# Spectral and dense layers on one core: another layout of a scratch tensor in memory, and an earlier place for one piece of the inverse transform

## The chip, the core and the metric

The kernel runs on one core of a Trainium2 chip. A core has five engines that run side by side and synchronise by semaphores: TensorE (PE, matrix products; its weight loads are shown apart as PEld), VectorE (DVE), ScalarE (ACT), GpSimd (POOL) and SyncE (SP), which only issues DMAs. Data move between the on-chip memory (SBUF, 128 partitions) and the main memory by 16 DMA engines; SP, ACT and POOL each have a queue to issue DMAs on. TensorE writes its results to PSUM, eight banks, from which DVE or ACT copy them out. The metric is the device time of one execution in microseconds; several executions are timed and the median is compared.

## What is computed

Two kinds of layer alternate, each twice: a spectral layer A and a dense layer B, both on a normalised input and added to it.

```python
def _A_ref(x, w_r, w_i):
    X = rfft2(x.astype(float32), axes=(-2, -1))
    X = X * (w_r + 1j * w_i)
    return irfft2(X, s=(S, D), axes=(-2, -1)).astype(bfloat16)

def _B_ref(x, w1, b1, w2):
    h = einsum("bsd,df->bsf", x, w1) + b1
    sp = log1p(exp(-abs(h))) + where(h > 0, h, 0)
    return einsum("bsf,fd->bsd", h * tanh(sp), w2)

x = A_x
x = x + _A_ref(_layernorm(x), A_w_r, A_w_i)
x = x + _B_ref(_layernorm(x), B_w1, B_b1, B_w2)
x = x + _A_ref(_layernorm(x), A_w_r, A_w_i)
x = x + _B_ref(_layernorm(x), B_w1, B_b1, B_w2)
```

S is 2048 rows, D 1024 columns, the hidden width of the dense layer 3584; data are bfloat16. `h * tanh(sp)` is the Mish function, which ACT computes in one instruction.

## The kernel before

**Order of work.** The program is written out by hand: each engine has one list of instructions, in the order in which the Python code adds them, and a helper (`op`, `group`, `dma`) works out which semaphores an instruction must wait for from the buffers that it reads and writes. An engine works strictly in its list's order, so an instruction that waits holds all that stand behind it, DMA issues included. The activations stay in SBUF (`XS`, 16 tiles of 128 rows).

**The spectral layer** (`layer_A`) computes both Fourier transforms as matrix products with constant tables. After a first stage the frequencies are worked through in eight groups g; `order_A` gives the order of the stages of all groups, several groups in flight at once. For each group, s2 and s3 finish the forward transform and apply the filter, i1 and i2 begin the inverse one. i2 leaves the group's result in the buffer `U[g % 3]`: 128 partitions (index l, the place in a piece of 128 columns), and in each partition 16 components r by 128 values n. That is 4 KB per partition, 512 KB per group.

The last step of the inverse transform, `i4`, contracts over all 128 components (16 of each of the eight groups), so these must lie on partitions, and l and n in a partition. The turn from the one order to the other is made through main memory, by the scratch tensor `u_scratch` (`u_d`), made in `build` at L309:

- `u_turn` (L864 to L877) stores a group. Groups 0 to 6 go as a whole on SP's queue once both halves of i2 are done (L875); group 7 goes in two halves of eight components each on ACT's queue (L871), so that the first half is on its way while the second is computed.
- `u_back` (L886 to L890) reads a group back into `UT`, one component per partition: component r of group g comes to partition 8 r + g. It is issued on SP, one group behind the stores: after the store of group g, the load of group g - 1. The load of group 6 is issued at the first half of group 7 (L870).
- `u_last` (L892 to L901) reads group 7 back in six parts: the first half's eight components in two parts of 64 values of l on SP, the second half's in four parts of 32 values of l, in turn on ACT and SP. Each part waits for the store of its half.

In the layout before, `u_scratch` has the order (group, l, r, n): a store writes 4 KB (group 7: 2 KB) per partition in one contiguous piece, and a load gathers pieces of 128 values, 256 bytes, into each component's partition.

While group 7 makes this way, TensorE has only `spin(4, 0)` (L940), matmuls whose result isn't used, and `residual_first` (L998), which puts the first four tiles of `XS` into PSUM. Behind the loads on SP stand the first loads of the dense layer's weights (`load_w1`, L1041), which wait for `UT` to be complete.

**The dense layer** (`layer_B`) starts with i4. For the first four row tiles, four calls of 32 values of l each (L1186; matmuls of 128x32, line L1014) add to the residual in PSUM, `out_first` (L1019) copies the sums to `XS` on ACT, and DVE takes the statistics of the normalisation. For the other twelve row tiles the work is cut into small pieces: `rest(bank, n)` (L1168) makes n matmuls of 128x96 (also line L1014) into PSUM banks from `bank` on, and one copy from there to the staging buffer `YS`, on ACT (line L568) unless told otherwise. These pieces stand between the dense layer's own matmuls. The first tiles are normalised (`apply`, L505, on DVE), transposed on TensorE (`transposed`, L1056: eight transposes at L1069 into bank 6 or 7, one copy out on DVE at L1074), and multiplied with w1 (`mm1`, L1088, matmuls at L1103 into banks 0 to 2), with the Mish on ACT (L1107). `self.warm(ACT.Mish)` (L1198) is a tiny activation whose purpose is to load ACT's table for Mish early. The second product, with w2, is `mm2` (L1113, line L1121).

The order at the start of the dense layer is: `rest(0)`, two `apply`, two `transposed`, the warming of the table, `rest(3)`, and further on the first `mm1`.

Of the kernel before, what the change touches and what calls it, by code (L numbers as in the profile page):

```python
# [7 lines left out]
P = 128  # L8
BF = dt.bfloat16
# [165 lines left out]
def to_bf16_bits(a):  # L175
    u = np.ascontiguousarray(a, dtype=np.float32).view(np.uint32).astype(np.uint64)
    return np.ascontiguousarray((((u + 0x7FFF + ((u >> 16) & 1)) >> 16) & 0xFFFF).astype(np.uint16))


class KB:  # L180
# [122 lines left out]
    def build(self):  # L303
        nc = self.nc
        tabs = make_tables()
        con = {k: nc.inline_tensor(to_bf16_bits(v), name=f"c_{k.lower()}") for k, v in tabs.items()}
        self.con = {k: v.ap().bitcast(BF) for k, v in con.items()}
        self.con["IDF"] = nc.inline_tensor(np.eye(P, dtype=np.float32), name="c_idf").ap()
        self.u_d = nc.dram_tensor("u_scratch", (8, P, 16, P), BF, kind="Internal").ap()  # L309
        self.w_d = nc.dram_tensor("w_scratch", (8, P, 2, 2, 512), BF, kind="Internal").ap()  # L310
        self.xn_d = nc.dram_tensor("xn_scratch", (16, P, self.D), BF, kind="Internal").ap()
        from contextlib import ExitStack
        with ExitStack() as es:
            def sb(name, shape, dtype=BF):
                return es.enter_context(nc.sbuf_tensor(name, [P] + shape, dtype))

            sb("PAD0", [64])
            self.XS = sb("XS", [16, self.D])
            self.IDENT = sb("IDENT", [P])
            self.M = sb("M", [P])  # L320
            self.MT = sb("MT", [P])
            self.FD = sb("FD", [5 * 512])
            self.BD = sb("BD", [13 * P])
            self.B1 = sb("B1", [self.NF], F32)
            self.B1h = sb("B1h", [self.NF])
            self.BN = sb("BN", [16, 12], F32)
            self.MV = sb("MV", [16, 2], F32)
            self.RS = sb("RS", [4, 16], F32)
            self.EPS = sb("EPS", [32], F32)
            sb("PAD1", [32])  # L330
            self.PS = es.enter_context(nc.psum_tensor("PS", [P, 8, 512], F32))
            self.PSb = self.PS[:].bitcast(BF)
            self.arena_bytes = nc.sbuf_bytes_remaining // 64 * 64 - 64
            self.ARENA = es.enter_context(nc.sbuf_tensor("ARENA", [P, self.arena_bytes // 2], BF))
            self.r_bank = [Res(f"bank{i}") for i in range(8)]
            self.r_xs = [Res(f"XS{i}") for i in range(16)]
            self.r_mv = [Res(f"MV{i}") for i in range(16)]
            self.r_rs = [Res(f"RS{i}") for i in range(16)]
            self.r_ident, self.r_m, self.r_mt, self.r_fd, self.r_bd = (Res(n) for n in ("id", "m", "mt", "fd", "bd"))
            self.r_b1, self.r_eps, self.r_warm = Res("b1"), Res("eps"), Res("warm")  # L340
            self.r_ud = [Res(f"ud{i}") for i in range(8)]
            self.r_ud7 = [Res(f"udh{i}") for i in range(2)]
            self.r_wd = [Res(f"wd{i}") for i in range(8)]
            self.r_xnd = [Res(f"xnd{i}") for i in range(16)]
            self.npair = 0
            self.W1_OFF = self.arena_bytes - 4 * 4096
            self.layout()
            self.prologue()
            self.layer_A(0)
            self.layer_B(0, last=False)  # L350
            self.layer_A(1)
            self.layer_B(1, last=True)
            self.dma_wait_all()
            for p in (self.pe, self.dve, self.act, self.sp, self.pool):
                p.sem = es.enter_context(nc.semaphore(name=f"sem_{p.name}"))
            for d_ in self.dsems.values():
                d_.sem = es.enter_context(nc.semaphore(name=d_.name))
            self.block = es.enter_context(nc.Block())
            self.flush()
# [329 lines left out]
    def layer_A(self, li):  # L689
# [7 lines left out]
        dve, act, sp, pool = self.dve, self.act, self.sp, self.pool  # L697
# [166 lines left out]
        def u_turn(g, half):  # L864

            u = U[g % 3]
            if g == 7:
                h = slice(8 * half, 8 * half + 8)
                if half == 0:
                    u_back(6)  # L870
                self.dma(act, self.u_d[g][:, h, :], u.ap[:, h, :], f"uwh{half}", reads=[u.res], writes=[self.r_ud7[half]])  # L871
                if half:
                    u_last()
            elif half:
                self.dma(sp, self.u_d[g], u.ap, f"uw{g % 3}", reads=[u.res], writes=[self.r_ud[g]])  # L875
                if g:
                    u_back(g - 1)  # L877

        def open_ut():
            self.UT = self.alloc("UT", o["UT"], [P, P])  # L880

            self.r_ut = self.sub_res(self.UT, "ut", 4, o["UT"], P * P * 2)
            for r in self.r_ut:
                r.begin()

        def u_back(g):  # L886
            if self.UT is None:
                open_ut()
            self.dma(sp, self.UT.ap[g:P:8, :, :], self.u_d[g].rearrange("l r n -> r l n"), f"usp{g % 3}",
                     reads=[self.r_ud[g]], parts=self.r_ut)  # L890

        def u_last():  # L892

            def back(prog, half, q, n):
                l = slice(32 * q, 32 * q + 32 * n)
                self.dma(prog, self.UT.ap[7 + 64 * half:P if half else 64:8, l, :], self.u_d[7][l, 8 * half:8 * half + 8, :].rearrange("l r n -> r l n"),
                         f"ul{half}{q}", reads=[self.r_ud7[half]], parts=self.r_ut[q:q + n])
            back(sp, 0, 0, 2)
            back(sp, 0, 2, 2)
            for q in range(4):  # L900
                back((act, sp)[q % 2], 1, q, 1)  # L901
# [147 lines left out]
    def layer_B(self, li, last):  # L1049
        pe, dve, act, sp, pool = self.pe, self.dve, self.act, self.sp, self.pool  # L1050
# [117 lines left out]
        def rest(bank, n=15, prog=act):  # L1168

            u0 = self.u0  # L1170
            self.u0 += n
            self.i4(4, 12, u0, n, bank)
            self.i4_out(4, 12, u0, n, bank, staged=YS, prog=prog)
# [17 lines left out]
            self.out_first(u, 2, (act, act, act, dve)[u])  # L1191
        self.root(0, 2)
        rest(0)
        for j in range(2):
            xn[j] = self.apply(j)
        for j in range(2):
            transposed(0, j, xn[j])
        self.warm(ACT.Mish)  # L1198
        rest(3)
        at_tiles(0)  # L1200
        for j in (2, 3):
            self.stats_dve(j)
# [118 lines left out]
```

## Time and profile before

| | us |
|---|---|
| median of 8 runs | 1014.73 |
| fastest and slowest of them | 1014.37, 1015.99 |
| the profiled execution, as timed | 1014.61 |
| its span from the first to the last instruction | 1012.8 |
| PE busy in it | 958.5 (95%) |
| ACT, DVE, POOL busy | 347.6, 326.6, 81.7 |
| first spectral layer's last i4 input landed, about | 114.5 |
| second spectral layer's, about | 604.9 |

How the scratch tensor's DMAs stand in the page (engine whose queue issues them, number, size of each, median time from issue to landing):

```profile
u_scratch<-ARENA SPq DMA_DIRECT2D x14, 512.0 KB, 4.0
ARENA<-u_scratch SPq DMA_DIRECT2D x14, 512.0 KB, 6.1
...
u_scratch<-ARENA ACTq DMA_DIRECT2D x4, 256.0 KB, 3.9
```

`ARENA` is the one SBUF tensor in which all buffers of the layers lie, `U` and `UT` among them. In the timelines a row gives start, duration, engine, line, operation, tiles, shapes and number of instructions, and in brackets how long the engine was idle before it and what ended the wait. In the chain of waits each piece is followed back from what came last. Rows on stretches of time give the busy time of each engine in the stretch, the clock that was granted to TensorE as a share of the full one, the busy share of the DMA engines (packets can overlap, so it can pass 1) and the rate in GB/s.

### The profile page before, as it was taken

The page shows a single profiled execution, that of the slowest core. Times are in us where ns is not written, and L with a number is a line of the kernel's source. Part 1 is how long each engine was busy: PE and PEld are TensorE (multiplying, and loading weights), DVE is VectorE, ACT ScalarE, POOL GpSimd, SP SyncE. Part 2 cuts the span into 40 slices and gives each one's busy share as a digit, 9 for nine tenths or more (in the row PEclk, how much of TensorE's full clock was granted, in tenths as well). Part 3 has the DMA queues.
Part 4 walks back from the last instruction along what each step waited for, and adds up shares of the span by engine and source line. Part 5 has one row for each costly group of instructions (what it writes and reads, how often), then busy time and mean ns, then how long its engine had stood idle before and what let it go on. Part 6 is the DMA issues. An engine that isn't in the chain of part 4 may idle for free.

```text
span 1012.8 us, 13752 instructions
## 1 busy us (share of the span) xinstructions
PE 958.5 (95%) x5826; PEld 506.8 (50%) x5826; DVE 326.6 (32%) x679; ACT 347.6 (34%) x487; POOL 81.7 (8%) x114
## 2 busy tenths in 40 slices
PE   1799799999999999999999979999999999999998
PEld 0676575444444444444456748644444444444443
DVE  6797468002443000033347736820011100000111
ACT  7898474330000334300029837533100023430000
POOL 4831000000000000003421100000000000000000
PEclk9999899999999999999999998999999999999999
DMA  9969813662111220002922875246411212100000
GB/s 284 295 187 319 216 47 115 208 197 55 46 46 32 81 75 21 1 21 93 194 57 90 237 178 152 78 163 201 129 25 48 70 52 83 43 1 11 21 27 26
DMA packets 154205, 107.00 MB, mean 106 GB/s; under 512 B 74448, under 2 KB 133664, under 8 KB 154144
## 3 DMA queue, kind: packets, MB, share of 16 engines
q1 hardware_dynamic: 143056, 78.61, 27.4%
q0 software_dynamic: 8912, 25.84, 8.6%
q10 hardware_dynamic: 2176, 1.66, 0.5%
q8 instruction: 47, 0.77, 0.3%
q14 instruction: 14, 0.11, 0.0%
HBM read 80.85 MB, written 20.71 MB: 100 GB/s over the span
## 4 chain that ended last, share of the span: by engine, by line
PE 87%; DVE 5%; DMA 4%; ACT 3%; issue 0%; SPq 0%; POOL 0%; ACTq 0%; DVEq 0%
PE PS L1121 38%; PE PS L1103 38%; PE PS L793 2%; PE PS L719 2%; PE PS L1014 2%; PE PS L818 2%; DMA ARENA<-c_bt 1%; ACT ARENA L441 1%; DMA ARENA<-u_scratch 1%; PE PS L1069 1%; DVE ARENA L637 1%; DMA u_scratch<-ARENA 1%; DMA XS<-in_A_x_dram 1%; DVE ARENA L610 1%; DVE ARENA L775 1%; ACT ARENA L635 1%
## 5 line engine op out<-in xcount | busy, mean ns | idle before, releaser
L1103 PE MATMUL PS<-ARENA 128*128 128x512 bf16 (+1 forms) x1984 | 390.9, 358 | 0.1
L1121 PE MATMUL PS<-ARENA 128*128 128x512 bf16 x1792 | 387.4, 379 | 0.0
L1107 ACT ACTIVATE ARENA<-PS,B 128x512 bf16<-128x512 f32 (+1 forms) x248 | 159.3, 645 | 411.5 <-PE PS L1103 411.0
L1103 PEld LDWEIGHTS PS<-ARENA 128*128 128x128 bf16 x1984 | 193.1, 98 | 192.5 <-DVE ARENA L1074 0.7
L1121 PEld LDWEIGHTS PS<-ARENA 128*128 128x128 bf16 x1792 | 175.3, 98 | 211.5
L1132 DVE TENSOR_TENSOR XS<-PS,XS 128x512 bf16<-128x512 f32 x63 | 43.6, 692 | 582.1 <-PE PS L1121 582.1
L460 DVE BATCH_NORM_STATS2 BN<-XS 128x6 f32<-128x512 bf16 x99 | 63.8, 674 | 5.4 <-DMA XS<-in_A_x_dram 4.3
L249 POOL DMA_DIRECT2D xn_scratch<-ARENA x12 | 6.5, 541 | 373.7 <-DVE ARENA L512 373.7
L793 PE MATMUL PS<-ARENA 128*128 128x256 bf16 x256 | 32.4, 273 | 4.0 <-DVE ARENA L782 3.2
L771 ACT ACTIVATE ARENA<-PS 128x1024 bf16<-128x1024 f32 x32 | 33.3, 1071 | 4.5 <-PE PS L767 4.5
L432 ACT ACTIVATE RS<-MV,EPS 128x2 f32<-128x2 f32 (+2 forms) x5 | 1.5, 298 | 96.6 <-DVE MV L463 84.4
L719 PE MATMUL PS<-FD,ARENA 128*128 128x256 bf16 (+1 forms) x256 | 31.8, 271 | 2.4 <-ACT ARENA L635 1.2
L1014 PE MATMUL PS<-MT,ARENA 128*128 128x32 bf16 (+1 forms) x512 | 22.3, 202 | 10.5 <-DMA ARENA<-u_scratch 7.2
L804 ACT ACTIVATE ARENA<-PS 128x1024 bf16<-128x1024 f32 x28 | 29.8, 1089 | 3.9 <-PE PS L793 3.9
L793 PEld LDWEIGHTS PS<-ARENA 128*128 128x128 bf16 x256 | 24.0, 98 | 12.1 <-DVE ARENA L782 5.8
L568 ACT ACTIVATE ARENA<-PS 128x1440 bf16<-128x1440 f32 (+1 forms) x22 | 25.5, 1160 | 11.0 <-PE PS L793 3.9
L775 DVE TENSOR_TENSOR ARENA<-ARENA 128x1024 bf16<-128x1024 bf16 x32 | 22.0, 688 | 21.2 <-ACT ARENA L771 21.2
L719 PEld LDWEIGHTS PS<-FD,ARENA 128*128 128x128 bf16 x256 | 24.4, 98 | 6.5 <-DVE ARENA L637 1.4
L1014 PEld LDWEIGHTS PS<-MT,ARENA 128*128 128x128 bf16 x512 | 20.8, 104 | 13.4 <-issue 7.9
L818 PE MATMUL PS<-ARENA,BD 128*128 128x256 bf16 x192 | 24.9, 273 | 1.6 <-DVE ARENA L572 1.6
L862 ACT ACTIVATE ARENA<-PS 128x1024 bf16<-128x1024 f32 x24 | 25.3, 1093 | 0.0
L512 DVE TENSOR_SCALAR ARENA<-XS,MV,RS 128x1024 bf16<-128x1024 bf16 x47 | 24.5, 546 | 0.9
(85 smaller groups left out, 531.3 us busy)
## 6 DMA issues: line engine op xcount, KB each, us to landing
ARENA<-in_B_w_dram SPq DMA_DIRECT2D x56, 512.0 KB, 3.9
ARENA<-in_B_w_dram SPq DMA_DIRECT2D x56, 256.0 KB, 4.3
u_scratch<-ARENA SPq DMA_DIRECT2D x14, 512.0 KB, 4.0
ARENA<-u_scratch SPq DMA_DIRECT2D x14, 512.0 KB, 6.1
w_scratch<-ARENA POOLq DMA_DIRECT2D x8, 512.0 KB, 7.0
ARENA<-w_scratch POOLq DMA_DIRECT2D x8, 512.0 KB, 5.4
out_dram<-XS SPq DMA_DIRECT2D x16, 256.0 KB, 2.0
ARENA<-xn_scratch POOLq DMA_DIRECT2D x15, 256.0 KB, 9.4
```

What stands on the lines that cost most here:

```text
L460: self.op(self.dve, lambda e: e.bn_stats(self.BN[:, j, 6 * h:6 * h + 6], self.XS[:, j, 512 * h:512 * h + 512]), reads=[self.r_xs[j]], part ...
L719: fns.append(lambda e: e.matmul(dst, at(r), FD[:, t:t + n], start=start, stop=stop))
L771: self.op(act, lambda e: e.activation(x.ap.rearrange("p a b -> p (a b)"), ps, ACT.Copy, scale=SIG), reads=banks, writes=[x.res])
L775: self.op(dve, lambda e: e.tensor_tensor(ta.ap, x.ap, wt.ap[:, 0:1, :].to_broadcast([P, 2, 512]), ALU.mult), reads=[x.res, wt.res], writes ...
L793: fns.append(lambda e, c=c, part=part: e.matmul(ps[:, c * 256:(c + 1) * 256], yk.ap[:, part, c * P:(c + 1) * P], t[:, (128, 0)[part]:(384, ...
L804: self.op(act, lambda e: e.activation(v.ap[:, :, i, :], src, ACT.Copy), reads=banks, parts=[v.res])
L818: fns.append(lambda e, dst=dst, part=part, c=c: e.matmul(dst, BD[:, c:c + P], mov(kd, part), start=(part == 0), stop=(part == 1)))
L1014: fns.append(lambda e, l=l: e.matmul(self.PS[:, bank + l // k, l % k * w:(l % k + 1) * w], self.UT.ap[:, u0 + l, :], self.MT[:, 8 * lo:8 * ...
L1103: fns.append(lambda e, db=db, bank=bank, fl=fl: e.matmul(PS[:, bank, 0:w], wb.ap[:, db, fl * P:(fl + 1) * P], x.ap[:, db, tok], start=(db ...
L1107: self.op(act, lambda e, bank=bank, ft=ft: e.activation(at.ap[:, ft, tok], PS[:, bank, 0:w], ACT.Mish, bias=self.B1[:, ft:ft + 1]), reads= ...
L1121: fns.append(lambda e, i=i, ft=ft: e.matmul(PS[:, bank, :], at.ap[:, ft, t * P:(t + 1) * P], W2[ft].ap[:, h * 512:(h + 1) * 512], start=(i ...
L1132: self.op(dve, lambda e: e.tensor_tensor(xs, PS[:, bank, :], xs, ALU.add), reads=[self.r_bank[bank]], writes=[self.r_xs[j]])
```

## The change

The scratch tensor gets the order (group, r, l, n): a component's row is contiguous in memory, 32 KB. The stores now scatter each partition's 4 KB (group 7: 2 KB) in pieces of 256 bytes, and the loads read one contiguous piece per component: 32 KB for groups 0 to 6, and for group 7's parts 16 KB (64 values of l) or 8 KB (32 values). Queues, order, waits and the number of DMAs stay as they are. Besides, in the dense layer one `rest(3)` moves from behind the transposes and the warming of the Mish table to a place right behind `rest(0)`.

```diff
@@ build
-        self.u_d = nc.dram_tensor("u_scratch", (8, P, 16, P), BF, kind="Internal").ap()
+        self.u_d = nc.dram_tensor("u_scratch", (8, 16, P, P), BF, kind="Internal").ap()
@@ u_turn
-                self.dma(act, self.u_d[g][:, h, :], u.ap[:, h, :], f"uwh{half}", reads=[u.res], writes=[self.r_ud7[half]])
+                self.dma(act, self.u_d[g][h].rearrange("r l n -> l r n"), u.ap[:, h, :], f"uwh{half}", reads=[u.res], writes=[self.r_ud7[half]])
...
-                self.dma(sp, self.u_d[g], u.ap, f"uw{g % 3}", reads=[u.res], writes=[self.r_ud[g]])
+                self.dma(sp, self.u_d[g].rearrange("r l n -> l r n"), u.ap, f"uw{g % 3}", reads=[u.res], writes=[self.r_ud[g]])
@@ u_back
-            self.dma(sp, self.UT.ap[g:P:8, :, :], self.u_d[g].rearrange("l r n -> r l n"), f"usp{g % 3}",
+            self.dma(sp, self.UT.ap[g:P:8, :, :], self.u_d[g], f"usp{g % 3}",
                      reads=[self.r_ud[g]], parts=self.r_ut)
@@ u_last
-                self.dma(prog, self.UT.ap[7 + 64 * half:P if half else 64:8, l, :], self.u_d[7][l, 8 * half:8 * half + 8, :].rearrange("l r n -> r l n"),
+                self.dma(prog, self.UT.ap[7 + 64 * half:P if half else 64:8, l, :], self.u_d[7][8 * half:8 * half + 8, l, :],
                          f"ul{half}{q}", reads=[self.r_ud7[half]], parts=self.r_ut[q:q + n])
@@ layer_B
         self.root(0, 2)
         rest(0)
+        rest(3)
         for j in range(2):
             xn[j] = self.apply(j)
         for j in range(2):
             transposed(0, j, xn[j])
         self.warm(ACT.Mish)
-        rest(3)
         at_tiles(0)
```

## The prediction

> **What bounds the kernel now.** I read first where the chain that ended last spends its time.
>
> ```profile
> PE 87%; DVE 5%; DMA 4%; ACT 3%; issue 0%; SPq 0%; POOL 0%; ACTq 0%; DVEq 0%
> ```
>
> TensorE is the chain for 87% of the span; what is not TensorE lies mostly in the two spectral layers. The diff touches what their ends hang on: the scratch tensor between L871/875 and L889/896, and the start of the next stage. So I read the chain in order of time there, first layer, then second:
>
> ```profile
> 104.89 3.71 DMA u_scratch<-ARENA
> 108.62 0.67 SPq L249
> 109.34 0.59 SPq L249
> 109.97 4.48 DMA ARENA<-u_scratch
> 114.59 2.63 PE PS L1014 x96
> ```
>
> ```profile
> 596.12 4.01 DMA u_scratch<-ARENA
> 600.15 4.74 DMA ARENA<-u_scratch
> 605.03 3.59 PE PS L1014 x128
> ```
>
> The whole machine waits for group 7's trip through memory: 9.7 us from the first store's issue at 104.89 to 114.59, and 8.9 us from 596.12 to 605.03 (the first store there is issued at 595.06). TensorE has only the spin and the residual matmuls (L646, L1003) to fill it. Next I cut the trip into stretches (time, then busy time of PE, PEld, DVE, ACT and POOL, the granted clock, the busy share of the DMA engines, GB/s):
>
> ```profile
> 100.70:102.30 1.60, 1.00 (x8) 0.70 (x8) 1.14 (x3) 0.28 (x1) 0.00 (x0) 1.00 1.03 307
> 592.80:594.00 1.20, 0.71 (x7) 0.64 (x8) 0.49 (x2) 0.34 (x1) 0.00 (x0) 1.00 1.27 290
> 594.00:596.80 2.80, 2.01 (x28) 1.20 (x25) 1.32 (x2) 1.19 (x2) 0.00 (x0) 1.00 1.24 210
> 106.80:108.60 1.80, 1.74 (x5) 0.53 (x5) 0.00 (x0) 0.00 (x0) 0.00 (x0) 1.00 0.94 303
> 598.70:600.20 1.50, 1.50 (x5) 0.42 (x3) 0.00 (x0) 0.00 (x0) 0.00 (x0) 1.00 0.05 18
> 601.20:604.80 3.60, 0.00 (x0) 0.00 (x0) 0.00 (x0) 0.00 (x0) 0.00 (x0) 0.92 0.64 130
> ```
>
> Row 1 is group 6's store in 4 KB pieces. Rows 2 and 3 are the loads of groups 5 and 6, whose packets are all under 512 B: 290 GB/s at first, then 210. Row 4 is both stores of group 7 (2 KB pieces), which hardly move before 106.8 because group 6's load holds the engines. Row 5 is a straggler: a few packets hold the second layer's stores for 1.5 us. Row 6 is group 7's loads, at 130 GB/s, with the engines only 0.64 busy: each writes eight partitions. The last view is the start of the dense stage, TensorE's timeline:
>
> ```profile
> 118.88 1.38 PE L1014 MATMUL PS<-MT,ARENA 128*128 128x96 bf16 x15 [1.67 <-ACT XS L568]
> 120.44 1.89 PE L1069 MATMUL PS<-IDENT,ARENA 128*128 128x128 bf16 x16 [0.18 <-DVE ARENA L512]
> 122.12 1.19 PE L1014 MATMUL PS<-MT,ARENA 128*128 128x96 bf16 x15
> 123.14 1.91 PE L1103 MATMUL PS<-ARENA 128*128 128x256 bf16 x16
> ```
>
> The second L1014 row is the piece that moves. It now fills the time in which VectorE copies the second transpose out (L1074, 122.36 to 123.05).
>
> **The change, part by part, per layer.** The bytes stay the same; the short pieces (256 B) move from the loads to the stores, and the loads get pieces of 32 KB, 16 KB or 8 KB.
>
> *Group 6's store (SP).* 512 KB take 1.6 us (row 1). No row has 256 B writes into memory, so I bound it by 256 B loads: 1.8 us at 290 GB/s, 4.0 us at 130; the other end is no loss. Row 2 is nearest, since its loads too reach the engines at full share: 1.8 us, +0.2. Queued behind it on SP: group 6's load waits for it, and group 7's loads stand behind that.
>
> *Loads of groups 5 and 6 (SP).* 1 MB from 102.5 to 106.8, 4.3 us. At row 1's rate 3.2 us; at row 3's 210 GB/s throughout 5.0 us. I take 3.9, since the first 1.2 us already run near 290: -0.4. What comes free is the way for group 7's stores.
>
> *Group 7's stores (ACT).* Issue: a store takes 0.33 us on ACT, a load in 256 B pieces 0.58 on SP, so +0.25 for the first and about +0.4 for the second, as ACT's copy at 105.28 sits between. Hidden now: the first store starts moving 1.9 us after its issue, group 6's store 0.9 us after. If that cover goes, it costs the 0.25 to 0.4. Data: 1.8 us now, 1.8 at 290 GB/s, 4.0 at 130; I take +0.1. In the second layer row 5's straggler adds 1.5 us; it follows a load in 256 B pieces that one engine ends late. With long pieces it may vanish (-1.2) or stay, or come from the scattered stores (0); I take -0.7.
>
> *Group 7's loads (SP and ACT).* 512 KB in 3.6 to 3.8 us. They still write eight partitions each, so about half of the engines: half of row 1's rate is 154 GB/s, 3.4 us; half of the 406 GB/s that the input loads reach at 3 to 4 us is 203, 2.6 us; the other end is no gain. I take 3.0, -0.8. SP's four issues of about 0.6 us shrink towards a plain store's 0.32, so the last starts earlier: -0.2 more.
>
> *Overlap.* In the first layer 32 of the 128 matmuls of L1014 run before the last load lands (112.59), in the second none. Shorter late loads should let some of those 0.95 us in: -0.4 in the second layer (0 to -0.95).
>
> *Groups 0 to 5.* Stores +0.2, loads -0.2 each, beside TensorE: nothing. The cover is the ring of three U buffers; without it, the table loads on POOL's queue come later (TensorE waits 0.8 us for one of them now).
>
> *The moved piece.* 15 matmuls with their weight loads and one ScalarE copy move ahead of 2 x 8 transposes; no DMA moves. TensorE has 0.18 us free there and the piece takes 0.64 us at full clock, 0.98 at the half clock granted here, so the transposes come 0.5 to 0.8 us later, the second copy with them, and the first L1103 matmul starts at about 123.7 with TensorE idle in front of it. On ScalarE the piece's copy (1.4 us) goes in front of the Mish table load (1.28 us), which had been hidden under the transposes; it still ends near 124.6, when the first Mish input is ready. Some comes back: at 127.44 TensorE waits 0.28 us for a copy that is now done earlier. Bounds 0 to +0.8, taken +0.4.
>
> **Sum.** First layer: 0.2 - 0.4 + 0.1 - 1.0 + 0.4 = -0.7. Second: the same -0.7, less 0.7 and 0.4: -1.8. Together -2.5. The profiled execution took 1014.61 us (span 1012.8 and 1.8 around it), so 1012.1; the median of the runs, 1014.73, lies 0.1 higher: **1012.2 us**.
>
> [...]
>
> **Rivals.**
>
> *Scattered stores are slow* (the slower side). Place: group 6's and 7's stores, 1 MB on the chain per layer. For it: nothing in the profile writes memory in pieces below 2 KB, and loads in 256 B pieces sank from 290 GB/s to 210 and 130. Against: 256 B is no handicap in row 2. At 130 GB/s the two take 8.0 us in place of 3.4, 4.3 more than my +0.3 per layer: 1012.2 + 8.6 = 1020.8; at 170, 2.5 more: 1017.2. It decides from 1 MB in 4.95 us (3.4 + 0.3 + 1.25), about 210 GB/s: there the gain is gone.
>
> *The loads don't get faster*, held by the partitions that they write, or because the long pieces are cut up again and the change doesn't do what it says. For it: row 3 and row 6 are below row 2 with the same pieces. Then -0.4 and -0.8 fall away twice: 1014.6, no change.
>
> *The granted clock comes back late.* It is 0.50 from 116.2 to 122.9 and from 604.1 to 614.2, and rises 4 us after 118.88 and 610.27, from where TensorE works nearly without a gap. The moved piece opens a gap of 0.7 to 0.9 us in just that stretch. The two cold stretches last 6.7 and 10.1 us, 3.4 apart; if the clock rises 3.4 us later, the dense matmuls lose 1.7 us per layer, the piece its full 0.8: +2.1 per layer, 1016.4.
>
> *Everything at the long pieces' rate*: loads of groups 5 and 6 at 3.2 us (-0.7 more), group 7's at 2.6 (-0.4), straggler gone (-0.5): 1012.2 - 2.7 = 1009.5.
>
> **Chances.** Forecast 0.42 (own range 1010.8 to 1013.8), slow stores 0.27, everything fast 0.12, loads unchanged 0.10, late clock 0.09. About 0.2%, 2.0 us, is what a measurement of this kernel tells from no change, so faster means below 1012.7 and slower above 1016.8. Faster: 0.28 of the forecast, 0.12, 0.01 of the unchanged loads: 0.41. Slower: 0.26 of the slow stores, 0.07 of the clock, 0.04 of the unchanged loads, 0.02 of the forecast: 0.39. The rest, 0.20, is no change. The range runs from 1010.0, which leaves out part of the fast case, to 1019.5, which leaves out stores below about 145 GB/s.
>
> **What would show it.** In the changed profile: the store of group 6 at 290 GB/s and landed about 3.3 us after its issue (now 3.1), or far below; the loads of group 7 in packets of several KB, over in 3 us; L1014's first matmuls about 1 us earlier after group 7's store issue; the first L1103 about 0.5 us later after the first L1014 of 96 columns; the clock back within 5 us of that. I am wrong if stores in 256 B pieces run below 210 GB/s, or if the loads stay near 130.

## The result and the profile after

The changed kernel takes 1020.89 us (median of 11 runs, 1018.26 to 1023.3); the kernel before, timed beside it, 1015.29 (31 runs). The ratio is 1.0055, with a 95% interval from 1.0046 to 1.0064: slower, by 5.6 us, and above the forecast's range. The profiled execution took 1019.02 us (span 1017.2), near the fastest of its runs. It is set against the 1014.61 us (span 1012.8) of the profile before.

First the page after, in the same parts as before: the chain by engine, two groups of instructions (number, busy time, mean ns, idle time in front and what ended it), and the scratch tensor's DMAs.

```profile
PE 86%; DMA 4%; DVE 4%; POOL 2%; ACT 2%; issue 1%; SPq 0%; ACTq 0%; DVEq 0%; POOLq 0%
...
L1103 PE MATMUL PS<-ARENA 128*128 128x512 bf16 (+1 forms) x1984 | 390.9, 358 | 2.0 <-DVE ARENA L1074 1.9
...
L1014 PE MATMUL PS<-MT,ARENA 128*128 128x32 bf16 (+1 forms) x512 | 20.0, 197 | 15.3 <-DMA ARENA<-u_scratch 11.9
...
u_scratch<-ARENA SPq DMA_DIRECT2D x14, 512.0 KB, 5.4
ARENA<-u_scratch SPq DMA_DIRECT2D x14, 512.0 KB, 7.3
```

L1014 waits 11.9 us for the loads of the scratch tensor, where it waited 7.2. Both DMAs are slower from issue to landing: the stores by 1.4 us, and also the loads, whose pieces became 128 times longer, by 1.2. The long pieces were not cut up: the page counts 381 DMA packets of 8 KB and more, the page before 61, and the 320 more are one for each row that the loads of the scratch tensor read.

The chain of waits after, first layer and second, answers to the two chains of the prediction:

```profile
107.13 6.87 DMA u_scratch<-ARENA
...
114.02 3.91 DMA ARENA<-u_scratch
...
118.17 3.59 PE PS L1014 x128
```

```profile
599.97 5.10 DMA u_scratch<-ARENA
...
605.09 4.95 DMA ARENA<-u_scratch
...
610.17 3.59 PE PS L1014 x128
```

These start at group 7's second store. From the issue of its first store (106.02 and 598.87) to the end of the 128th i4 matmul the trip takes 15.73 and 14.87 us; before it took 12.32 and 13.54. That is 3.4 and 1.3 us more. In the first layer 32 of the 128 matmuls no longer run ahead of the last load. Of the 4.4 us between the two spans, 1.1 arise before the first trip, in work that the change doesn't touch (such starts differ from run to run: group 7's first store is issued at 104.27 us in run 4, at 106.74 in run 8), and 4.7 in the two trips; 0.7 us per layer come back behind them. There the clock returns to full, in the first layer, 0.6 us after the end of the 128th matmul (at 122.4), before 5.7 us after it (at 122.9); that this is what brings the time back is likely, but no run separates it.

Rates in stretches of the trip after (columns as in the prediction):

```profile
595.00:596.60 1.60, 1.05 (x8) 0.70 (x8) 1.06 (x3) 0.25 (x1) 0.00 (x0) 1.00 1.24 281
601.00:602.60 1.60, 1.57 (x4) 0.53 (x5) 0.00 (x0) 0.00 (x0) 0.00 (x0) 1.00 0.82 152
602.60:604.80 2.20, 2.03 (x5) 0.42 (x3) 0.00 (x0) 0.00 (x0) 0.00 (x0) 1.00 0.63 143
605.50:609.60 4.10, 0.00 (x0) 0.00 (x0) 0.00 (x0) 0.00 (x0) 0.00 (x0) 0.69 0.54 128
```

Row 1 is group 6's store in 256 B pieces: 281 GB/s, near the 290 that the prediction took. In rows 2 and 3 group 7's stores move, at 152 and 143 GB/s, but this is not the rate of 256 B pieces. Such a row counts a packet, its bytes and its busy time, whole in the stretch in which it starts, and a 32 KB packet of the changed loads lasts about 2.2 us (median). Group 6's load, issued at 597.50, lands 6.0 us later; its packets that started before 601.00 hold engines in row 2 and are not counted there. From 602.60 to 603.50 the stores alone move at 269 GB/s, and from 603.50 to 604.80, while the last engines finish, at 55. Row 4 is group 7's loads, now in pieces of 8 and 16 KB: 128 GB/s, where 256 B pieces had 130. Long pieces gained nothing.

The busy tenths of the DMA engines in 40 slices of 0.7 us, from 84 to 112 us, before and after, counted in the same way:

```profile
DMA  9999998996999999999899849999999999800355
```

```profile
DMA  9924799996019981975069999900899940699077
```

Before, the engines were nearly full until group 7's trip. After, the zeros look like holes, but they stand behind slices in which 32 KB packets start, and such a packet covers three slices. With each packet's time spread over the slices that it covers, the engines are 0.85 full or more after as well, but for three slices (0.5 from 89.6 to 90.3 us, 0.2 and 0.4 from 94.5 to 95.9). So what the stores wait for is engines that are busy. Group 6's store shows it: issued at 100.94, it lands 5.9 us later, where it took 3.1 before (second layer 3.6 for 3.0), and from 101.5 to 103.5 the engines spend 0.95 of their time on 32 KB packets of group 4's load, which lands at 105.5.

The issue of the DMAs changed too. Durations of the issuing instructions (shortest, median, longest, in ns), before, after, and then in two of the runs below, run 3 (contiguous stores, long loads) and, its last line alone, run 4 (scattered stores, short loads):

```profile
L249 SPq DMA_DIRECT2D ARENA<-u_scratch x22: 537/580/1362, 67.2 to 601.4; - x22
...
L249 ACTq DMA_DIRECT2D u_scratch<-ARENA x4: 326/333/383, 104.9 to 596.1; - x4
```

```profile
L249 SPq DMA_DIRECT2D ARENA<-u_scratch x22: 477/1104/3987, 68.5 to 606.0; - x22
...
L249 ACTq DMA_DIRECT2D u_scratch<-ARENA x4: 372/670/2130, 106.0 to 600.0; - x4
```

```profile
L249 SPq DMA_DIRECT2D ARENA<-u_scratch x22: 477/527/1183, 67.8 to 602.7; - x22
L249 ACTq DMA_DIRECT2D u_scratch<-ARENA x4: 332/876/1535, 104.8 to 597.3; - x4
...
L249 SPq DMA_DIRECT2D ARENA<-u_scratch x22: 519/972/4321, 66.9 to 603.2; - x22
```

A load on SP stands right behind a store, and its issue, 0.58 us before (median; at most 1.36), now takes up to 3.99 us; ACT's second store of group 7 takes up to 2.13. The two have different causes. SP's long issues come with the scattered stores: up to 4.32 us in run 4, not above 1.18 in run 3. ACT's come with the long loads, even where the store itself is contiguous: 1.42 and 1.53 us in run 3 (1.75 and 2.45 in run 11, 1.46 and 2.17 in run 17), but 0.37 and 0.76 in run 4. That either costs time isn't shown. SP's load of group 4 is held from 96.86 to 100.48, but group 6's store, next on SP, is issued 5.08 us ahead of group 7's first, as before (5.07); and in run 3 group 7's second store lands 3.06 and 4.19 us after its issue (3.19 and 4.01 before), held or not.

### The profile page after: what moved, and what is told of

Same layout as the page of the kernel before. It is cut to its first block, busy times and chain, and to the rows that moved or that the text cites. A ratio compares the mean times of both kernels' runs of the same rounds, so it can differ in the third digit from the quotient of the medians.

```text
span 1017.2 us, 13752 instructions
## 1 busy us (share of the span) xinstructions
PE 955.8 (94%) x5826; PEld 504.3 (50%) x5826; DVE 326.6 (32%) x679; ACT 347.8 (34%) x487; POOL 81.9 (8%) x114
## 4 chain that ended last, share of the span: by engine, by line
PE 86%; DMA 4%; DVE 4%; POOL 2%; ACT 2%; issue 1%; SPq 0%; ACTq 0%; DVEq 0%; POOLq 0%
PE PS L1121 38%; PE PS L1103 38%; PE PS L793 2%; PE PS L719 2%; PE PS L1014 2%; PE PS L818 2%; POOL ARENA L610 1%; DMA u_scratch<-ARENA 1%; DMA XS<-in_A_x_dram 1%; DMA ARENA<-u_scratch 1%; POOL ARENA L249 1%; DMA ARENA<-in_A_w_i_dram 1%; PE PS L1069 1%; PE PS L850 1%; DVE ARENA L775 1%
## 5 line engine op out<-in xcount | busy, mean ns | idle before, releaser
L1103 PE MATMUL PS<-ARENA 128*128 128x512 bf16 (+1 forms) x1984 | 390.9, 358 | 2.0 <-DVE ARENA L1074 1.9
L1103 PEld LDWEIGHTS PS<-ARENA 128*128 128x128 bf16 x1984 | 192.9, 98 | 194.8 <-DVE ARENA L1074 2.9
L1014 PE MATMUL PS<-MT,ARENA 128*128 128x32 bf16 (+1 forms) x512 | 20.0, 197 | 15.3 <-DMA ARENA<-u_scratch 11.9
L1014 PEld LDWEIGHTS PS<-MT,ARENA 128*128 128x128 bf16 x512 | 18.9, 101 | 18.0 <-issue 13.7
```

Source lines behind the costliest of these rows:

```text
L1014: fns.append(lambda e, l=l: e.matmul(self.PS[:, bank + l // k, l % k * w:(l % k + 1) * w], self.UT.ap[:, u0 + l, :], self.MT[:, 8 * lo:8 * ...
L1103: fns.append(lambda e, db=db, bank=bank, fl=fl: e.matmul(PS[:, bank, 0:w], wb.ap[:, db, fl * P:(fl + 1) * P], x.ap[:, db, tok], start=(db ...
```

## The experiments

All are compared with the kernel before on the same chip. "Trip" is, in one profiled execution, the time from the issue of group 7's first store to the end of the 128th i4 matmul, first and second layer; the sum of the two goes with the ratio, to about 1.5 us. Runs 3, 7, 8 and 17 leave out the turn of the components, so they tell times and nothing else.

| kernel | median us | ratio to before (95%) | trips, us |
|---|---|---|---|
| before | 1015.29 | 1 | 12.32, 13.54 |
| changed kernel | 1020.89 | 1.0055 (1.0046 to 1.0064) | 15.73, 14.87 |
| 1 layout only | 1020.03 | 1.0046 (1.0029 to 1.0063) | 15.23, 15.87 |
| 2 moved piece only | 1015.44 | 1.0001 (0.9992 to 1.0010) | 11.84, 13.05 |
| 3 long pieces both ways | 1016.59 | 1.0015 (1.0007 to 1.0024) | 13.54, 13.98 |
| 4 short pieces both ways | 1018.73 | 1.0031 (1.0022 to 1.0040) | 13.98, 14.06 |
| 5 group 7 only | 1017.94 | 1.0024 (1.0015 to 1.0033) | 13.82, 14.19 |
| 6 groups 0 to 6 only | 1016.84 | 1.0015 (1.0006 to 1.0024) | 14.01, 13.72 |
| 7 stores in 512 B | 1016.04 | 1.0007 (0.9998 to 1.0017) | 13.35, 13.03 |
| 8 stores in 1 KB | 1015.99 | 1.0007 (0.9996 to 1.0017) | 12.25, 13.41 |
| 9 other partitions of UT | 1026.22 | 1.0112 (1.0096 to 1.0129) | 21.82, 17.03 |
| 10 load of group 5 earlier | 1016.25 | 1.0015 (1.0004 to 1.0025) | 12.96, 13.07 |
| 11 group 6 only | 1016.84 | 1.0015 (1.0004 to 1.0026) | 12.71, 13.14 |
| 12 group 6's store on ACT | 1017.33 | 1.0025 (1.0015 to 1.0036) | 14.17, 13.72 |
| 13 sixteen partitions | 1011.58 | 0.9962 (0.9947 to 0.9976) | 10.86, 11.40 |
| 14 the same, new layout | 1016.49 | 1.0003 (0.9991 to 1.0014) | 13.17, 12.03 |
| 15 stores in halves, new layout | 1017.79 | 1.0022 (1.0009 to 1.0035) | 14.64, 13.95 |
| 16 sixteen and halves | 1011.78 | 0.9957 (0.9943 to 0.9970) | 10.16, 11.12 |
| 17 sixteen, long pieces both ways | 1011.86 | 0.9965 (0.9951 to 0.9978) | 10.78, 11.37 |
| 18 sixteen and halves, new layout | 1014.83 | 0.9994 (0.9986 to 1.0003) | 12.79, 12.09 |

### Which half of the change: 1 and 2

Run 1 is the changed kernel with `rest(3)` back at its old place; run 2 is the kernel before with `rest(3)` moved.

```diff
# run 1, against the changed kernel
         rest(0)
-        rest(3)
...
         self.warm(ACT.Mish)
+        rest(3)
# run 2, against the kernel before
         rest(0)
+        rest(3)
...
         self.warm(ACT.Mish)
-        rest(3)
```

> The changed layout of the scratch tensor alone; the inverse piece stays behind the transposes. Theory S (the scattered stores start late and land late, and all of the loss is the layout's): +4.5 to +6.5 us against the kernel before, and group 7's stores take 5 to 7 us from the second one's issue to its landing, as in the changed kernel (6.9 and 5.1). Rival R (the moved piece carries part of the loss, at the +0.4 per layer of the prediction): about 1 us less than the changed kernel.

> The moved inverse piece alone, with the old layout. Theory S: between -1.5 and +1 us, that is nothing that can be told from no change. Rival R: +1 to +2 us. In the trace TensorE should wait 0.7 to 0.9 us for the second transposed copy in front of the first 128x256 matmul.

The layout carries the loss, and the piece is worth nothing that can be told: 1.0001, at most 1.0 us. It does open the gap that was forecast. TensorE's timeline in run 2, first layer:

```profile
119.20 1.45 PE L1014 MATMUL PS<-MT,ARENA 128*128 128x96 bf16 x30 [1.67 <-ACT XS L568]
120.76 1.08 PE L1069 MATMUL PS<-IDENT,ARENA 128*128 128x128 bf16 x16
122.77 1.92 PE L1103 MATMUL PS<-ARENA 128*128 128x256 bf16 x16 [0.93 <-DVE ARENA L1074]
```

TensorE stands for 0.93 us in front of L1103, with the copy L1074 late. From the first piece to L1103 it is 3.57 us here, at the full clock, and 4.82 in the second layer, at the half clock; before it was 4.26 and 4.33. The two layers differ more by the clock than by the order.

### Stores or loads: 3, 4, 7 and 8

Run 3 leaves the stores contiguous and gives the loads long pieces; run 4 scatters the stores and reads back in 256 B pieces, which lie 512 B apart. Runs 7 and 8 store in pieces of 512 B and 1 KB and read in 256 B.

```diff
# run 3, loads of groups 0 to 6; group 7's alike
-  self.u_d[g].rearrange("l r n -> r l n")
+  self.u_d[g].rearrange("(r a) b n -> r (a b) n", r=16)
# run 4, beside the new layout
-  "u_scratch", (8, 16, P, P)
+  "u_scratch", (8, 16, P, 2, P)
# run 7 (m = 2) and run 8 (m = 4), stores
-  self.u_d[g], u.ap
+  self.u_d[g].rearrange("(r l n) -> l r n", l=P, n=m * P), u.ap.rearrange("l (r m) n -> l r (m n)", m=m)
```

> Stores contiguous as before (4 KB and 2 KB pieces) and loads in 32, 16 and 8 KB pieces, piece at the old place: the loads take the bytes in the order in which they lie, so the components come mixed up and the turn is left out. Theory S (only the scattered stores cost): as fast as the kernel before or up to 3 us faster. Rival L (the long loads hold the DMA engines, and group 7's stores wait behind group 6's load): +2 to +5 us, with the stores of group 7 landing 5 us or more after their issue although they go in long pieces.

> Stores scattered in 256 B pieces as in the changed kernel, but every piece lies 512 B from the next, so that the loads too go in 256 B pieces as in the kernel before; piece at the old place. Theory S: +4 to +8 us. Rival L: within 1.5 us of the kernel before, since no long load holds an engine.

> The stores scatter pieces of 512 B in place of 256 B, half as many; the loads gather 256 B pieces as in the kernel before (from where the bytes lie, so components come mixed up and the turn is left out); piece at the old place. Theory N (the time goes with the number of pieces): half of what the 256 B stores with short loads cost (+3.7 us), so +1.5 to +2.3. Rival T (a threshold at 512 B, below which a write is dear): within 0.8 us of the kernel before. Rival Z (scattering as such is dear, whatever the piece): +3 us or more.

> The same with stores in pieces of 1 KB, a quarter as many as in the changed kernel; the turn is left out. Theory N: +0.5 to +1.2 us. Rival T: within 0.8 us of the kernel before, and the same as with 512 B. Rival Z: +3 us or more.

The two halves add up: 3.1 per mille for the scattered stores and 1.5 for the long loads (each to about 0.9) against 4.6 for both (to 1.7). So neither theory held whole: S had the long loads at no cost; L had the scattered stores within 1.5 us, and the long loads holding up group 7's stores, which land in run 3 within 0.3 us of before. What run 3's profile shows in place of a gain is that the 32 early matmuls are lost and that the load takes 5.14 and 5.01 us in the chain, for 4.48 and 4.74. The term that was to bring the gain, the loads, is a loss of its own. In the stores the piece's size decides: 3.1 per mille at 256 B, 0.7 at 512 B and 0.7 at 1 KB. Scattering as such, whatever the piece, would have left all of it, and falls. A cost in proportion to the number of pieces would have left 1.6 and 0.8; 0.7 at 512 B lies low for that, but the interval (-0.2 to 1.7) doesn't exclude it, so a step between 256 and 512 B and a cost per piece are not told apart.

### Which groups: 5, 6 and 11

Run 5 gives the new order to group 7 alone, run 6 to groups 0 to 6, run 11 to group 6 alone, each with a scratch tensor of its own beside the other.

```diff
# run 5 (run 6 the other way round)
+  self.u7_d = nc.dram_tensor("u7_scratch", (16, P, P), BF, kind="Internal").ap()
-  self.dma(act, self.u_d[g][:, h, :], ...
+  self.dma(act, self.u7_d[h].rearrange("r l n -> l r n"), ...
-  self.u_d[7][l, 8 * half:8 * half + 8, :].rearrange("l r n -> r l n")
+  self.u7_d[8 * half:8 * half + 8, l, :]
# run 11
+  self.u6_d = nc.dram_tensor("u6_scratch", (16, P, P), BF, kind="Internal").ap()
-  self.dma(sp, self.u_d[g], u.ap, ...
+  self.dma(sp, self.u6_d.rearrange("r l n -> l r n") if g == 6 else self.u_d[g], u.ap, ...
```

> Only group 7's scratch has the new order; groups 0 to 6 and the moved piece are as before. Theory S1 (the scattered stores of group 7 land late by themselves): +3 to +5 us. Rival S2 (it is the scattered stores of the groups before that fill the DMA queues, so that group 7's stores stand behind them): within 1 us of the kernel before.

> Groups 0 to 6 in the new order, group 7 and the piece as before. Theory S1: +0 to +1.5 us, and group 7's stores land 3 to 4 us after their issue, as before (3.2 and 4.0). Rival S2: +3 to +5 us.

> Group 6 alone in the new order (store in 256 B pieces, load in 32 KB pieces); groups 0 to 5 and 7 as before. Groups 0 to 6 together cost 1.5 per mille. Theory S (the store of group 6 itself starts late on SP, and only it lies on the chain): 1.0 to 1.5 per mille, 1016.0 to 1016.6, its store landing in 4.5 to 5.5 us. Theory B (the stores of groups 3 to 5 and the loads behind them arrive late and pass the delay on): within 0.5 per mille, the store of group 6 landing in 4 us or less.

Both parts lose, 2.4 and 1.5 per mille, so neither S1 nor S2 is the whole. In run 5 group 7's stores do run fast:

```profile
107.40:109.40 2.00, 1.95 (x5) 0.67 (x6) 0.00 (x0) 0.00 (x0) 0.00 (x0) 1.00 1.21 256
601.00:602.80 1.80, 1.80 (x5) 0.56 (x4) 0.00 (x0) 0.00 (x0) 0.00 (x0) 1.00 1.16 255
```

At 255 GB/s a store in 256 B pieces is far above the 130 that the slow-store rival took; the 143 to 152 of the changed kernel come when group 6's load ahead of it is in 32 KB pieces. Part of run 5's loss lies in the loads: 5.02 and 4.92 us from issue to landing in its chain, for 4.48 and 4.74 before, and the 32 early matmuls wait for the end. Run 11 stays undecided: its ratio is that of theory S, but group 6's store lands in 3.5 us, as theory B has it, and its profiled execution shows a trip as short as before.

### SP's queue: 10, 12 and 15

Run 10 is the kernel before with group 5's load moved ahead of group 6's store. Runs 12 and 15 are the new layout with `rest(3)` at its old place: in 12 group 6's store is issued on ACT, in 15 groups 0 to 6 are stored in two DMAs of eight components.

```diff
# run 10
-                if g:
+                if g and g != 6:
                     u_back(g - 1)
+            elif g == 6:
+                u_back(5)
# run 12
-  self.dma(sp, self.u_d[g].rearrange("r l n -> l r n"), u.ap, ...
+  self.dma(act if g == 6 else sp, self.u_d[g].rearrange("r l n -> l r n"), u.ap, ...
# run 15, at each half of a group
+  h = slice(8 * half, 8 * half + 8)
+  self.dma(sp, self.u_d[g][h].rearrange("r l n -> l r n"), u.ap[:, h, :], ...
```

> The kernel before with one DMA issued earlier: the load of group 5 ahead of the store of group 6 on SP, at the first half of group 6, instead of behind it. If the long landing of group 7's stores comes from the loads of groups 5 and 6 that run ahead of them, it shortens: i4 starts 0.5 to 1.5 us earlier in at least one layer, 1013 to 1014.5. If SP's wait on the store of group 5 only moves the store of group 6 back, no change or up to 1 us slower.

> The new layout with the moved piece back at its old place (1020.0 us), and group 6's store issued on ACT's queue instead of SP's. Theory Q (256 B pieces are slow to start because SP's queue is still full of the work of earlier loads and stores): its data start within 1.5 us of the issue, group 6's load and so group 7's come 1 to 2 us earlier, 1018 or less. Theory W (the pieces themselves are slow, on any queue): issue to landing stays above 5 us, 1020 or, as ACT is held longer by the issue, up to 1021.

> The new layout (1020.0 us), and groups 0 to 6 stored in two DMAs of eight components (1024 pieces of 256 B each), the first already at the first half of the group. Theory Q (a store of 2048 pieces starts 2 to 4 us after its issue and blocks the load's issue behind it; in halves each is like group 7's, which started soon): group 6's second half lands in 4 us or less, 1017.5 to 1018.8. Theory W (the number of pieces on SP's queue sets it): no change, 1019.5 to 1021.

Run 10 gains nothing, and its ratio lies 1.5 per mille above: that order of DMAs ahead of group 7's stores was not what held the kernel before. Runs 12 and 15 each win back about half of the layout's loss, 2.1 and 2.4 of 4.6 per mille (from another set of runs, so not to the tenth). So a good part of the scattered stores' cost is where and in what portions they are queued, as theory Q has it. Its own detail was wrong, though: in run 12 group 6's store, alone on ACT's queue, still lands 7.0 and 5.6 us after its issue. In the first layer it is issued at 100.28 and starts near 102, and until then the engines are busy with 32 KB packets of group 4's load: the stretch from 100.00 to 102.00 reads 1.06 of the engines' time and 276 GB/s. Here an empty queue didn't help, with the engines behind it full.

### Why long pieces bring nothing: 9, 13, 14 and 17

Each of group 7's loads writes eight partitions and runs at 125 to 130 GB/s in both layouts. Run 9 puts the components on other partitions and reads every group in two DMAs of eight. Run 13 reads group 7 in DMAs of 16.

```diff
# run 9
-  self.UT.ap[g:P:8, :, :], self.u_d[g].rearrange("l r n -> r l n")
+  p0 = 64 * h + 32 * (g // 4) + g % 4          # h = 0, 1
+  self.UT.ap[p0:p0 + 29:4, :, :], self.u_d[g][:, 8 * h:8 * h + 8, :].rearrange("l r n -> r l n")
# run 13, u_last
-  def back(prog, half, q, n):
...
-  back(sp, 0, 0, 2)
-  back(sp, 0, 2, 2)
+  def back(prog, q):
+      l = slice(32 * q, 32 * q + 32)
+      self.dma(prog, self.UT.ap[7:P:8, l, :], self.u_d[7][l, :, :].rearrange("l r n -> r l n"),
+               f"ul{q}", reads=self.r_ud7, parts=self.r_ut[q:q + 1])
   for q in range(4):
-      back((act, sp)[q % 2], 1, q, 1)
+      back((sp, act)[q % 2], q)
# run 14, beside the new layout: the source in run 13's place
+      self.u_d[7][:, l, :]
# run 17, beside run 3's layout
+      self.u7_d.rearrange("h (r a) b n -> (h r) (a b) n", r=8)[:, l, :]
```

> The layout and the order of the kernel before, but the components lie on other partitions of UT: component r of group g on 64 (r // 8) + 32 (g // 4) + 4 (r % 8) + g % 4 in place of 8 r + g (the rows of MT permuted alike, so the output is the same), and each group is read back by two DMAs of eight components. Theory P (the loads are held by where their partitions lie, not by the length of their pieces): group 7's loads, 128 to 130 GB/s in both kernels, clearly faster, above 180 GB/s, their 3.6 us at most 2.6; about 1 us less in each spectral layer, median about 1013 (0.998). Theory L (held by something else that both layouts share, such as eight descriptors' targets at a time): group 7's loads stay at 120 to 140 GB/s, and the second DMA per group adds 0.5 us on SP, median 1015 to 1016.

> The kernel before; only group 7 is read back otherwise: four DMAs of all 16 components by 32 values of l (16 partitions each), in turn on SP and ACT, once both of its stores have landed, in place of two and four DMAs of eight components each. Theory R (the rate of a load follows the number of partitions that one DMA writes: 250 to 290 GB/s at 16, 126 to 144 at eight): group 7's loads pass 200 GB/s and take about 2.2 us instead of 3.6 to 3.8; they start up to 0.7 us later; 0.5 to 1.2 us less per layer, 1012.8 to 1014.3. Theory K (the loads at the end of the trip are slow for another reason, such as the fixed time of a DMA): still about 130 GB/s, and 0.5 us more per layer, 1016.

> The new layout (moved piece at its old place, 1020.0 us), and group 7 read back in four DMAs of 16 components as in the run before, here in pieces of 8 KB. Theory R: group 7's loads above 200 GB/s here too, 1018 to 1019; the rest of the loss, in the scattered stores, stays. If long pieces in themselves hold the loads: 126 to 140 GB/s as before, 1020 to 1021.

> Contiguous stores and long loads at once (the turn is left out, so components are mixed, as in the third run), with group 7 read back in four DMAs of 16 partitions, here in pieces of 8 KB. It tells what long load pieces are worth once partitions don't hold the loads: with group 7 in 256 B pieces the same reading gave 1011.6 us, 0.9962. Theory L2 (long pieces are then faster, as the forecast had it): 0.5 to 1.5 us better, 0.9950 or less. Theory M (long pieces are worth nothing, or cost a little as in the third run): 0.9960 to 0.9985, group 7's loads issued and landed in 2.6 us or more.

Run 9 lost 11 per mille, far more than either theory said. Its loads, all of eight partitions now, in a stretch where nothing else moves:

```profile
114.00:116.00 2.00, 0.00 (x0) 0.00 (x0) 0.00 (x0) 0.00 (x0) 0.00 (x0) 0.92 0.63 144
116.00:118.00 2.00, 0.00 (x0) 0.00 (x0) 0.00 (x0) 0.00 (x0) 0.00 (x0) 0.50 0.63 143
```

On other partitions, then, 144 GB/s at 0.63 of the engines' time (130 at 0.64 before, in row 6 of the prediction), and now groups 0 to 6 are read in DMAs of eight too, where before they had 210 to 290 in DMAs of 16. Theory P is out, and the count of partitions in one DMA was left as a candidate. Run 13 tried that. Its loads of group 7, and below the chain in the second layer (L1012 there is the line L1014 of the kernel before):

```profile
110.40:111.20 0.80, 0.64 (x2) 0.00 (x0) 0.00 (x0) 0.00 (x0) 0.00 (x0) 1.00 0.40 93
111.20:112.10 0.90, 0.00 (x0) 0.00 (x0) 0.00 (x0) 0.00 (x0) 0.00 (x0) 1.00 1.26 283
...
600.40:601.20 0.80, 0.00 (x0) 0.00 (x0) 0.00 (x0) 0.00 (x0) 0.00 (x0) 1.00 0.43 99
601.20:602.10 0.90, 0.00 (x0) 0.00 (x0) 0.00 (x0) 0.00 (x0) 0.00 (x0) 1.00 1.25 280
```

```profile
595.42 4.02 DMA u_scratch<-ARENA
...
599.51 2.67 DMA ARENA<-u_scratch
...
602.32 3.45 PE PS L1012 x128
```

The engines' busy share goes from 0.63 in run 9 to 1.26, and the rate doubles, from 144 to 283 GB/s. The load takes 2.67 us from issue to landing where it took 4.74, with 256 B pieces and the partitions as before. It waits for both stores, which comes about 0.5 us later in the first layer (4.2 us after the first store's issue for 3.7), and wins all the same: 3.6 us off the two trips, 0.9962 in time, faster than both kernels of this case. The rate is read straight from the rows; of the time, a part may come from the order, since now one DMA brings all that the first 32 matmuls need, and no run separates the two. Run 14 does it in the new layout: 184 GB/s rising to 279, and 1.0003 in place of 1.0046. Run 17 asks what was left of the forecast: with 16 partitions, and stores contiguous, long pieces (0.9965) and 256 B pieces (0.9962) are the same, to about 2 per mille (each interval reaches about 1.4 to either side, and the two come from different sets of runs); the trips agree to 0.1 us. That is theory M's range; theory L2's 0.9950 lies just beyond the end of run 17's interval. So once a DMA writes 16 partitions, no gain from longer load pieces is seen. That run 3's 1.5 per mille came from its loads of eight is likely, but it lies within this uncertainty.

### Together: 16 and 18

Run 16 is the kernel before with group 7 read in DMAs of 16 and all stores in halves; run 18 is the same in the new layout. Their diffs are those of runs 13 and 15, and of 14 and 15, put together.

> The layout before, with both: group 7 read back in four DMAs of 16 components, and groups 0 to 6 stored in two halves, the first as soon as it is computed. If group 6's store and load that run ahead of group 7's stores cost it 1 us and more, as the second layer's straggler of 1.5 us says, 0.3 to 1.0 us per layer better than the 16 components alone; if the DMA engines are full there anyway, as in the first layer, within 0.5 us of it.

> The new layout with both mends: group 7 read back in four DMAs of 16 components (alone 1.0003), and groups 0 to 6 stored in halves (alone 1.0022, 2.4 per mille better than the new layout). If the two gains add up, 0.9980. If the halves win only by shortening what the slow loads of group 7 waited for, 0.9995 to 1.0005. What is left to the layout before with the same two edits (0.9957) is the price of 256 B pieces in the stores.

Run 16 (0.9957) is not to be told from run 13 (0.9962), though its first trip is 0.7 us shorter. Run 18 lands at 0.9994, near the case in which the two gains don't add up. What stays between the layouts with both edits is 3.7 per mille, 3.8 us, from two sets of runs: the price of scattering the stores in 256 B, together with whatever the 32 KB loads of groups 0 to 6 cost, which no run here takes apart from it.

## Why the prediction was wrong

**Group 6's and 7's stores: the step that failed first.** Their bytes were priced by row 2, loads in 256 B pieces at 290 GB/s, as +0.2 and +0.1 us per layer. Scattering alone (run 4) costs 3.1 per mille, 3.2 us for the two layers instead of 0.6. The rate was about right where the store runs alone (281 GB/s for group 6, 255 for group 7 in run 5), though row 1 and row 4 include the start of the stores: 2 KB pieces move at 382 GB/s from 597.50 to 598.50, so group 7's bytes alone lose about 0.5 us per layer, not 0.1 (an estimate from 382 and 281 GB/s). What the step lacked is the wait for busy engines before the bytes move. Group 6's store was to land 3.3 us after its issue; it took 5.9 and 3.6 in the changed kernel, 5.5 and 3.3 in run 4. The issue, costed at +0.25 to +0.4 us, "hidden", is not where the time went: ACT's first store of group 7 is issued in 0.39 and 0.37 us for 0.34 and 0.33, and its second, up to 2.13, is held by the long loads, not by its own pieces.

**The loads: the step that failed as well.** Groups 5 and 6 (-0.4), group 7 (-0.8), its issues (-0.2) and the overlap (-0.4) were to bring 3.2 us over the two layers. Alone (run 3) they cost 1.5 per mille, 1.5 us. The prediction had the reason in hand: each of group 7's loads writes eight partitions, "so about half of the engines" (row 6 has 0.64 of their time), for which it worked out 154 GB/s and 3.4 us; then it took 3.0, halfway to the 2.6 us that half of the input loads' 406 GB/s would give. Runs 9 and 13 show the eight to be the limit: 144 GB/s at eight, 283 at 16, and run 14 and the changed kernel show the same with 8 and 16 KB pieces, 279 and 128. The 3.6 to 3.8 us did not shrink with the long pieces (at 126 and 128 GB/s, the 512 KB take 4.2 and 4.1 us), and the prediction's own sign of being wrong, loads that stay near 130, came true. SP's four issues of group 7's loads took 0.54 to 0.64 us, not 0.32. The overlap went the other way: the 32 early matmuls of the first layer were lost.

**The straggler** (-0.7): it didn't pay. The second store of the second layer lands 5.10 us after its issue for 4.01 before, and with long loads alone (run 3) 4.19. A slow end is still there: 55 GB/s, at 0.25 of the engines' time, from 603.50 to 604.80.

**The moved piece** (+0.4 per layer): its parts are there (the gap in front of L1103, the late L1074), its sum is not: 1.0001, interval 0.9992 to 1.0010, so +0.8 us is not excluded, nor is nothing.

**The rivals.** Slow stores, at 0.27, gave 1020.8 us and the median is 1020.89; that it comes so near is luck. It had 130 GB/s for all of 1 MB per layer, but the bytes ran at 255 to 281 where nothing held them, the time went into waiting, and a third of the loss is the loads'. That the loads don't get faster was true besides, so two rivals held at once, where the chances had them as alternatives. The late clock did not come: in both layers it is back within 1 us of where it was before, at 122.4 and 613.9 us for 122.9 and 614.5. Nor did it wait for TensorE to work without a gap, as that rival had it: at 122.4 TensorE stands idle, from 121.75 to 123.41.

**What stays open.** In the changed kernel the stores wait for engines that are busy with the loads ahead. Run 4, with short loads, lands group 6's store as late in the first layer (5.5 us), and there it isn't shown what the scattered pieces add. Nor is it shown why the next load's issue on SP is held behind a store in 256 B pieces, and whether the cost grows with the number of pieces or sets in below 512 B: SP's longest load issue is 4.32 us at 256 B (run 4), 1.13 at 512 B (run 7), 0.67 at 1 KB (run 8). Stores in pieces of 512 B and 1 KB leave 0.7 per mille of the cost, which may be nothing; another queue or smaller portions take back about half of the layout's (runs 12, 15).

## What to carry to other kernels

Count the rows that one DMA writes before pricing the length of its pieces: with eight rows the engines were busy for 0.63 of the time at 144 GB/s (run 9), with 16 for 1.26 at 283 (run 13), and the new layout left it so (128 GB/s in the changed kernel, 279 in run 14), while putting 16 rows into one DMA saved 3.8 per mille with no change of layout. Short pieces are not free to shift from the reading to the writing side: loads in 256 B pieces were as fast as long ones (0.9962 and 0.9965 in DMAs of 16, runs 13 and 17), stores in 256 B pieces cost 3.1 per mille, about 3 us (run 4), and in 512 B pieces 0.7 (run 7). A DMA's issue time and start are to be read together with the DMAs ahead of it, on other queues too: group 6's store, alone on ACT's queue in run 12, landed 7.0 us after its issue, with group 4's load on the engines. And a rate over a short stretch misleads where packets last longer than the stretch: in these rows a 32 KB packet, about 2.2 us long, counts only where it starts.

## What the runs showed of the hardware

Loads in DMAs of eight partitions ran at 125 to 144 GB/s and in DMAs of 16 at 279 to 295 in their steady part (runs 13 and 14), with pieces of 256 B and of 8 KB alike (at eight, of 16 KB too). The engines' busy share was 0.51 to 0.64 at eight and 1.08 to 1.26 at 16. Where the partitions lie made no difference of that size: eight of them eight apart ran at 125 and 130 GB/s (kernel before), eight of them four apart at 144 and 143 (run 9), and 16 of them eight apart at 283 and 280 (run 13). What makes the rate go with the count isn't shown.

Stores in 256 B pieces moved 255 to 281 GB/s where they ran alone; in the kernel before, 4 KB pieces moved 328 from 100.90 to 101.90 and 2 KB pieces 382 from 597.50 to 598.50. So the bytes move more slowly in 256 B pieces, but at more than half of either rate. In time, the scattered stores cost 3.1 per mille at 256 B (run 4), and 0.7 at 512 B and at 1 KB (runs 7 and 8); a step between 256 and 512 B fits that, and a cost per piece nearly does too.
